# Third token block of six MLP passes by seven half-width products, inverses for two groups, another order of the attention stage

## The chip, the cores and the metric

One core of a Trainium2 chip runs the whole program in one launch. The metric is device time in microseconds, the median of several runs. The profile is one execution of the same program, with its own time.

## The reference

Inputs are q, k, v (2 batches, 8 heads, 768 positions, 64 features each), and weights of two MLPs over 1536 tokens of width 512 with 2048 hidden features. All is float32.

```
k_sum, v_sum: maximum of k and mean of v over blocks of 32 positions
scores = concat(q k^T / 8 where |i - j| < 16 else -1e9,  q k_sum^T / 8 + log 32)
a = softmax(scores);  attn = a @ concat(v, v_sum)
x = attn as (1536 tokens, 512)
h = x @ w_in;   x = (max(h, 0) + alpha * min(h, 0)) @ w_out        # first MLP
h = x @ w_in2;  out = (h * sigmoid(h)) @ w_out2                    # second MLP
```

## The kernel before

**Numbers.** Every float32 operand of the MLPs is held as a high part and a low part (fp32r), and a product is three matmuls: low times high, high times low, high times high (`three`, lines 295 to 302). The weights arrive in a packed form and are turned into these parts by three VectorE bit operations (`bits`, L135 to L151), a ScalarE cast (`w_high`, L162) and a subtraction (`w_low`, L167).

**Stages.** The attention stage takes 24 groups, each one of six blocks of 256 tokens and one of four head pairs. Per group: scores (TensorE, L592), masking and scaling (VectorE, L604), the row maximum (L615), exponentials with row sums (ScalarE, L622), the inverse of the sums (L631 and L632), normalisation (GpSimd, L638), a transpose (TensorE, L644), its copy out of PSUM (L393), the product with the values (L661) and the split of the result into high and low parts (L686, L690). Per batch and head pair it also needs the block maximum of k (L512) with copies of it (L393), and the block means of v: for batch 1 a VectorE sum (`sum_v`, L528).

The MLP stage is eight passes: two layers of four chunks of 512 hidden features. Pass 1 works beside the attention stage, in blocks of 256 tokens. Passes 2 to 8 work on three blocks of 512 tokens. Two of the three take part in a product scheme with seven products in place of eight (`product`, L250 to L282): the contraction (512 features in 4 tiles) is cut in two, a pair of feature tiles is cut in two, and the two token blocks are the third cut. It needs sums of weight pieces (`combine`, L180, `sum_high`, `sum_low`) and sums of token pieces (`x_first` for layer 1, `x_again` for layer 2, cast at L244). Of its partial sums some are copied by ScalarE (`seed_c` L286, `keep` L290) and added by VectorE (`add_to`). The third block (`DIRECT_T`, block 0 in layer 1 and block 2 in layer 2) is computed without it: `direct` (L934) runs four feature tiles of 4 x 3 matmuls of 512 columns. After the activation (L325 and L335, or L341 for the second layer) and its split into high and low (L349, L170) come the output matmuls: `outs` (L988), 12 matmuls for each of four output tiles of a token block, with the running sum put into PSUM by ScalarE before (L417) and copied back after (L438).

**Order.** All instructions are ordered before the launch by `plan` (L1170): every step has an engine, a cost, steps it must follow, buffers it takes and gives, and a key. The planner places the step that can start first, and among those that can start within a small time of each other the one with the lowest key. Steps of the attention stage have keys from the group number and constants (`AT_...`), MLP steps have latest times worked out backwards from TensorE's own order (`late`, L1158). TensorE's MLP steps stand in a list (`line`) and may be moved past two others (`LOOK = 3`). Some steps may go to one of two engines, whichever ends first in the plan. Where the plan has a hole on TensorE early on, dummy matmuls are put in (`fill`, L472).

**Buffers that matter.** Two conversion tiles (`w`), twelve pairs of weight parts (`wt`), four pairs of weight sums (`sw`), seven temporaries (`tmp`), nine pairs of activation parts (`gg`), eight PSUM banks. The weight sums of a pass are given back when the products that read them are done.

The order of TensorE's work from pass 3 on in the kernel before, quoted from lines 1106 to 1112 (`f` is the first feature tile of the third block):

```
def quads(i, f=None, *a):
    for x in ((0, 0), (1, 0), (0, 1), (0, 2), (0, 5), (0, 3), (1, 1), (1, 2),
              (0, 6), (0, 4), (1, 5), (1, 3), (1, 6), (1, 4)):
        if f and x == (1, 5):
            f(*a)
        quad(i, *x)
```

Of the kernel before, what the change touches and what calls it, by code (L numbers as in the profile page):

```python
# [21 lines left out]
P = 128  # L22
# [14 lines left out]
SLACK, RATE = 0.0, 0.28  # L37
# [5 lines left out]
A_PS, A_SB, D_TT, D_STT, D_HALF = 0.5, 0.53, 0.61, 0.69, 0.36  # L43
EARLY, LOOK = {}, 3
NEAR, T_NEAR = {"PE": 0.5, "DVE": 0.2, "ACT": 0.15}, 100.0


@with_exitstack
def tile_blocks_attention_mlps(
# [61 lines left out]
    w_t, sums_t = {}, {}  # L111
# [10 lines left out]
    def temp(name):  # L122
        n = got.pop(0)
        pool, tag = (gpool[0], "mgs"[n]) if n < 3 else (gpool[1], f"t{n}")
        return pool.tile([P, 512], F32, tag=tag, name=name, bufs=1)

# [60 lines left out]

    def sum_high(i, kk, n, at):
        hi = wp2[0].tile([P, 512], F32R, tag="wh", name="sh")
        lo = wp2[0].tile([P, 512], F32R, tag="wl", name="sl")  # L190
        sums_t[i, kk, n] = hi, lo
        nc.scalar.copy(out=hi, in_=w_t[at])

    def sum_low(i, kk, n, at):
        hi, lo = sums_t[i, kk, n]
        less(lo, w_t[at], hi)
# [3 lines left out]
    def pair(l):  # L200
        t = TB * (1 - l)
        return slice(t, t + TB), slice(t + TB, t + 2 * TB)

    def place(l, kk, n):
        if n < 3:
            return tt[0][:, n, 0, kk], tt[0][:, n, 1, kk]
        t1 = pair(l)[1]
# [4 lines left out]
    def x_first(kk, j):  # L212
        t0, t1 = pair(0)
        k2 = kk + KT // 2
        if j == 0:
            for n, tag in enumerate(("wh", "wl", "wh")):
                x_t[kk, n] = wp2[0].tile([P, TB], F32, tag=tag, name="b")
        b11, b12, b22 = [x_t[kk, n] for n in range(3)]
# [11 lines left out]
    def x_again(kk, j):  # L230
        t0, t1 = pair(1)
# [4 lines left out]
    def x_source(l, kk, n):  # L236
        if l == 0:
            return x_t[kk, (0, 2, 1, 0)[n]]
        t0, t1 = pair(1)
# [3 lines left out]
    def x_sum_high(l, kk, n):  # L243
        nc.scalar.copy(out=place(l, kk, n)[0], in_=x_source(l, kk, n))  # L244

    def x_sum_low(l, kk, n):
        hi, lo = place(l, kk, n)
        less(lo, x_source(l, kk, n), hi)

    def product(i, q, n, st):  # L250

        l, ch = passes[i]
        c1, c2 = slice(q * P, (q + 1) * P), slice((q + 2) * P, (q + 3) * P)
        t0, t1 = pair(l)
# [4 lines left out]
        def s(kk, f, c):  # L259
            return tuple(x[:, c] for x in sums_t[i, kk, f])  # L260
# [4 lines left out]
        def t(kk, f):  # L265
            return tt[0][:, f, 0, kk], tt[0][:, f, 1, kk]
# [1094 lines left out]
```

## Time and profile before

| | |
|---|---|
| median of 3 runs | 588.88 us (588.14 to 590.24) |
| the profiled execution | 587.72 us, span 585.9 us |
| TensorE busy | 573.2 us, 98% of the span |
| VectorE busy | 398.2 us, 68% |
| ScalarE busy | 353.4 us, 60% |
| GpSimd busy | 57.3 us, 10%, all before 130 us |
| TensorE clock granted | 1.000 in the mean |

Times in the rows are microseconds from the start of the span. PE is TensorE, PEld its weight loads, DVE VectorE, ACT ScalarE, POOL GpSimd. Durations of matmuls overlap in the trace, so the time that one costs in a stream is read from the starts of two of them.

### The profile page before, as it was taken

The page shows a single profiled execution, that of the slowest core. Times are in us where ns is not written, and L with a number is a line of the kernel's source. Part 1 is how long each engine was busy: PE and PEld are TensorE (multiplying, and loading weights), DVE is VectorE, ACT ScalarE, POOL GpSimd, SP SyncE. Part 2 cuts the span into 40 slices and gives each one's busy share as a digit, 9 for nine tenths or more (in the row PEclk, how much of TensorE's full clock was granted, in tenths as well). Part 3 has the DMA queues.
Part 4 walks back from the last instruction along what each step waited for, and adds up shares of the span by engine and source line. Part 5 has one row for each costly group of instructions (what it writes and reads, how often), then busy time and mean ns, then how long its engine had stood idle before and what let it go on. Part 6 is the DMA issues. An engine that isn't in the chain of part 4 may idle for free.

```text
span 585.9 us, 9240 instructions
## 1 busy us (share of the span) xinstructions
PE 573.2 (98%) x3535; PEld 481.2 (82%) x3535; DVE 398.2 (68%) x711; ACT 353.4 (60%) x781; POOL 57.3 (10%) x64
## 2 busy tenths in 40 slices
PE   8999899999999999999999999999999999999997
PEld 6778778999888888888888788888888888888886
DVE  4889999559999878984799969364657357404110
ACT  3788977436567557654757766436655575646442
POOL 2447644310000000000000000000000000000000
PEclk9999999999999999999999999999999999999999
DMA  8967843200220431242024112240132204000112
GB/s 245 300 212 217 233 136 110 74 1 1 72 73 0 142 110 37 72 148 68 2 78 136 38 37 72 73 143 1 36 109 79 65 0 117 28 1 0 73 54 91
DMA packets 23517, 51.04 MB, mean 87 GB/s; under 512 B 2224, under 2 KB 11696, under 8 KB 23472
## 3 DMA queue, kind: packets, MB, share of 16 engines
q1 hardware_dynamic: 23472, 50.44, 28.4%
q8 instruction: 28, 0.46, 0.3%
q14 instruction: 17, 0.14, 0.1%
HBM read 47.29 MB, written 3.15 MB: 86 GB/s over the span
## 4 chain that ended last, share of the span: by engine, by line
PE 81%; DVE 10%; DMA 4%; ACT 2%; issue 1%; POOL 1%; SPq 0%; ACTq 0%; DVEq 0%
PE ps L298 26%; PE ps L300 26%; PE ps L299 26%; DVE w L146 2%; DMA vs<-in_vw 1%; DMA y<-in_w 1%; DVE nm L615 1%; DVE t L604 1%; PE o L661 1%; DMA cst<-in_consts 1%; DVE w L140 1%; DVE xl L170 1%; DMA kT<-in_kT 1%; PE pt L644 1%; DVE tt L170 1%
## 5 line engine op out<-in xcount | busy, mean ns | idle before, releaser
L170 DVE TENSOR_TENSOR gl<-g,gh 128x512 fp32r<-128x512 f32 x72 | 48.6, 690 | 89.6 <-ACT gh L349 89.2
L298 PE MATMUL ps<-xh,wl 128*128 128x512 f32 (+1 forms) x292 | 104.8, 359 | 1.3 <-ACT ps L286 0.7
L299 PE MATMUL ps<-xl,wh 128*128 128x512 f32 (+1 forms) x292 | 103.4, 354 | 0.0
L300 PE MATMUL ps<-xh,wh 128*128 128x512 f32 (+1 forms) x292 | 103.4, 354 | 0.0
L438 ACT COPY y<-ps 128x512 f32<-128x512 f32 (+1 forms) x81 | 47.2, 582 | 83.1 <-PE ps L300 82.7
L146 DVE SCALAR_TENSOR_TENSOR w<-raw,w 128x512 uint32<-128x512 uint32 x116 | 82.0, 707 | 3.4
L298 PE MATMUL ps<-gh,wl 128*128 128x512 f32 (+1 forms) x240 | 83.6, 348 | 0.6 <-ACT pT L393 0.5
L299 PE MATMUL ps<-gl,wh 128*128 128x512 f32 (+1 forms) x240 | 83.3, 347 | 0.0
L300 PE MATMUL ps<-gh,wh 128*128 128x512 f32 (+1 forms) x240 | 83.2, 347 | 0.0
L299 PE MATMUL ps<-wl,gh 128*128 128x512 f32 (+1 forms) x196 | 75.4, 385 | 0.0
L300 PE MATMUL ps<-wh,gh 128*128 128x512 f32 (+1 forms) x196 | 75.4, 385 | 0.0
L298 PE MATMUL ps<-wh,gl 128*128 128x512 f32 (+1 forms) x196 | 75.4, 385 | 0.0
L298 PEld LDWEIGHTS ps<-xh,wl 128*128 128x128 f32 x292 | 55.1, 189 | 10.8 <-POOL wl L167 1.1
L300 PEld LDWEIGHTS ps<-xh,wh 128*128 128x128 f32 x292 | 55.1, 189 | 7.6
L299 PEld LDWEIGHTS ps<-xl,wh 128*128 128x128 f32 x292 | 55.2, 189 | 7.5
L162 ACT CAST wh<-w 128x512 fp32r<-128x512 f32 x64 | 39.2, 621 | 23.0 <-DVE w L146 22.9
L167 DVE TENSOR_TENSOR wl<-w,wh 128x512 fp32r<-128x512 f32 x54 | 37.1, 693 | 22.6 <-ACT wh L162 21.7
L298 PEld LDWEIGHTS ps<-gh,wl 128*128 128x128 f32 x240 | 45.4, 189 | 6.7 <-ACT pT L393 0.7
L299 PEld LDWEIGHTS ps<-gl,wh 128*128 128x128 f32 x240 | 45.4, 189 | 5.8
L300 PEld LDWEIGHTS ps<-gh,wh 128*128 128x128 f32 x240 | 45.4, 189 | 5.6
L349 ACT CAST gh<-g 128x512 fp32r<-128x512 f32 x72 | 43.5, 621 | 6.5 <-DVE g L335 5.3
L299 PEld LDWEIGHTS ps<-wl,gh 128*128 128x128 f32 x196 | 36.8, 188 | 7.4
(104 smaller groups left out, 962.2 us busy)
## 6 DMA issues: line engine op xcount, KB each, us to landing
raw<-in_w SPq DMA_DIRECT2D x58, 512.0 KB, 3.5
vs<-in_vw SPq DMA_DIRECT2D x16, 288.0 KB, 6.1
kT<-in_kT SPq DMA_DIRECT2D x8, 480.0 KB, 6.3
q<-in_qT SPq DMA_DIRECT2D x24, 128.0 KB, 4.6
y<-in_w SPq DMA_DIRECT2D x6, 512.0 KB, 5.0
out<-y SPq DMA_DIRECT2D x11, 256.0 KB, 2.0
raw<-in_vT SPq DMA_DIRECT2D x4, 384.0 KB, 5.3
cst<-in_consts SPq DMA_DIRECT2D x1, 348.0 KB, 4.9
```

What stands on the lines that cost most here:

```text
L140: nc.vector.tensor_scalar(out=w_t[n], in0=high, scalar1=3, scalar2=0x3FFFFFFF, op0=ALU.logical_shift_left, op1=ALU.bitwise_and,)
L146: nc.vector.scalar_tensor_tensor(out=w_t[n], in0=in0, scalar=scalar, in1=w_t[n], op0=op0, op1=ALU.bitwise_or)
L162: nc.scalar.copy(out=hi, in_=w_t[n])
L167: eng.tensor_tensor(out=lo, in0=w_t[n], in1=hi, op=ALU.subtract)
L170: nc.vector.tensor_tensor(out=out, in0=a, in1=b, op=op)
L298: i = nc.tensor.matmul(ps, all_, bh, start=first, stop=False, skip_group_check=again)
L299: nc.tensor.matmul(ps, ah, bl, start=False, stop=False, skip_group_check=again)
L300: nc.tensor.matmul(ps, ah, bh, start=False, stop=last, skip_group_check=again)
L349: nc.scalar.copy(out=gh, in_=acts_t[u, f])
L438: nc.scalar.copy(out=out_at(u, m, h, halves), in_=out_ps[u, m, h][:, :u[3] // halves])
L604: nc.vector.scalar_tensor_tensor(out=t.rearrange("p (h i) c -> p h (i c)", h=2), in0=s_t.pop((blk, p))[:, :, :2 * NC], scalar=scale, in1=m ...
L615: nc.vector.tensor_reduce(out=nm, in_=t_t[blk, p], axis=AX.X, op=ALU.max, negate=True)
```

## The change

**Third block.** In passes 3 to 8 (`THIRD`) the third block of 512 tokens goes by the seven products as well: it is cut into two halves of 256 columns, which take the place of the two token blocks. There are two row pairs of feature tiles, called products 2 and 3 in `quad`. Pass 2 keeps `direct`. The token sums are formed a second time for the halves (`tt1`), at the start of each layer. Copies, adds and activations of these products are 256 wide; the split into high and low parts is again 512 wide.

**Weight sums.** They are now in use until the third block's products are done. Of the second of each pair of sums only one half has a buffer of its own (256 columns); the other half is written over a piece of the weights that no product reads.

**Order of TensorE.** The two row pairs of the third block stand in `alone`, with output groups between their products. The last output group of a pass (three of them at the change of layer) moves among the first products of the next.

**Buffers.** Temporaries 7 to 5, activation pairs 9 to 8; the activation of the first layer works in place.

**Attention.** From the fifth group on, the inverse of the row sums is taken for two groups at once (24 reductions and 24 reciprocals become 14 and 14). The block sum of v may run on GpSimd as five additions, and does so for three of the four. `PLACES` gives a key to each step of many classes (53 lists, up to 24 entries each) in place of the formula, and `ENGINE` fixes the engine of many steps that had a choice: all eight copies of the k maxima go to GpSimd, 14 copies of transposed scores to ScalarE and 6 to VectorE, the rest stay open.

The core of the diff (most of the two tables, the passing on of `third` and changed planner costs are left out):

```diff
+NTMP, NGG = 5, 8
+LAG = {"POOL": 0.1, "DVE": 0.03}
...
+PLACES = {
+    "k": (
...
+    "e": (
+        38.07, 61.03, -116.39, 46.01, 95.72, 20.52, -16.7, 5.24, -10.94, 41.76, 34.66, 72.25, 132.07, 21.46,
+        -21.38, -35.41, 336.4, 198.65, 371.54, -22.07, 18.91, 95.51, 226.45, 21.33,
+    ),
+    "pt": (
...
+ENGINE = {
+    ("K", "POOL"): (
+        0, 1, 2, 3, 4, 5, 6, 7,
+    ),
...
+    ("vr", "POOL"): (
+        0, 2, 3,
+    ),
+    ("vr", "DVE"): (
+        1,
+    ),
...
+        if n == 0:
+            hi = wp2[0].tile([P, 512], F32R, tag="wh", name="sh")
+            lo = wp2[0].tile([P, 512], F32R, tag="wl", name="sl")
+            sums_t[i, kk, n] = [(hi[:, h], lo[:, h]) for h in HALVES]
+            whole_t[i, kk] = hi, lo
+            nc.scalar.copy(out=hi, in_=w_t[at])
+            return
+        hi = wp2[0].tile([P, 256], F32R, tag="vh", name="sh")
+        lo = wp2[0].tile([P, 256], F32R, tag="vl", name="sl")
+        spare = tuple(x[:, HALVES[1]] for x in pieces[(*passes[i], 0, kk)])
+        sums_t[i, kk, n] = [(hi, lo), spare]
+        for (hi, _), h in zip(sums_t[i, kk, n], HALVES):
+            nc.scalar.copy(out=hi, in_=w_t[at][:, h])
...
+    def pair(l, third=0):
+        t, w = (2 * TB * l, TB // 2) if third else (TB * (1 - l), TB)
+        return slice(t, t + w), slice(t + w, t + 2 * w)
...
         l, ch = passes[i]
+        third, q = divmod(q, 2)
         c1, c2 = slice(q * P, (q + 1) * P), slice((q + 2) * P, (q + 3) * P)
-        t0, t1 = pair(l)
+        t0, t1 = pair(l, third)
...
+    def act_part(u, f, part):
+        if got:
+            acts_t[u, f] = temp("g")
+        return acts_t[u, f][:, part]
...
+            if eng is nc.vector:
+                nc.vector.tensor_reduce(out=t, in_=v, axis=AX.X, op=ALU.add)
+            else:
+                half, part = BLOCK // 2, kv.tile([P, NB, BLOCK // 2], F32, name="vp", bufs=1)
+                while half:
+                    to = part[..., :half] if half > 1 else t.unsqueeze(2)
+                    nc.gpsimd.tensor_tensor(out=to, in0=v[..., :half], in1=v[..., half:2 * half], op=ALU.add)
+                    half, v = half // 2, part
...
+        def inverse(groups, sm):
+            n = 4 * len(groups)
+            rs = att.tile([P, 8, 1], F32, tag="rs", name="rs", bufs=3)
+            r = rs.rearrange("p u o -> p (u o)")[:, :n]
+            at = 4 * sm[1]
+            nc.vector.tensor_reduce(out=r, in_=sm[0][:, at:at + n], axis=AX.X, op=ALU.add)
             nc.vector.reciprocal(out=r, in_=r)
-            sums[blk, p] = rs
+            for j, g in enumerate(groups):
+                sums[g] = rs[:, 4 * j:4 * j + 4]
...
+            twin = (k - SOLO) % 2 if k >= SOLO else 0
+            sm = eps[k // 2 % 3], k % 2
+            mate = order[k - 1] if twin else g
...
+            if k < SOLO:
+                step(("rs", *g), "DVE", 0.28, [("ex", *g)], k + AT_NORM, inverse, [g], sm)
+            elif twin:
+                step(("rs", *mate), "DVE", 0.3, [("ex", *mate), ("ex", *g)], k + AT_NORM, inverse, [mate, g], (sm[0], 0))
+            if k % 2:
+                freed[k // 2 % 3] = mate
...
+            wp2.append(ctx.enter_context(tc.tile_pool(name="wp2", bufs=CF // 2)))
             gpool.append(ctx.enter_context(tc.tile_pool(name="g2", bufs=2)))
-            tt.append(
-                ctx.enter_context(tc.tile_pool(name="tt", bufs=1)).tile([P, 3, 2, KT // 2, TB], F32R, name="tt")
-            )
+            rest = ctx.enter_context(tc.tile_pool(name="tt", bufs=1))
+            for third in range(2):
+                tt.append(rest.tile([P, 3, 2, KT // 2, TB // (1 + third)], F32R, name=f"tt{third}"))
...
+        THIRD = {i: int(i > 1) for i in range(len(passes))}
...
+        def quads(i, left=()):
+            left = dict(zip(((1, 5), (0, 5), (0, 2)), left))
             for x in ((0, 0), (1, 0), (0, 1), (0, 2), (0, 5), (0, 3), (1, 1), (1, 2),
                       (0, 6), (0, 4), (1, 5), (1, 3), (1, 6), (1, 4)):
-                if f and x == (1, 5):
-                    f(*a)
+                if x in left:
+                    outs(*left[x])
                 quad(i, *x)
+
+        def alone(i, q, t, m):
+            for part, order_ in enumerate(((0, 5), (1, 2, 6, 3), (4,))):
+                for n in order_:
+                    quad(i, q, n)
+                if part < 2:
+                    outs(i, t, m, fs=((0, CF // 2), (CF // 2, CF)), part=part)
 
         def some(i, t, *ms):
             for m in ms:
@@ -1118,36 +1417,32 @@
         quads(1)
         split_outs(1, 1)
         some(1, 1, 2, 3)
-        some(1, 2, *range(KT))
+        some(1, 2, *range(KT - 1))
+        left = [(1, 2, KT - 1)]
         for i in range(2, len(passes)):
-            d = DIRECT_T[i]
-            quads(i, direct, i, d, 0)
-            split_outs(i, int(d == 0))
-            if d == 0:
-                some(i, 1, 2)
-                direct(i, 0, 1)
-                some(i, 1, 3)
-                direct(i, 0, 2)
-                direct(i, 0, 3)
-                some(i, 2, 0)
-                some(i, 0, *range(KT))
-                if i == NCH - 1:
-                    token_sums(1)
-                some(i, 2, *range(1, KT))
+            l = passes[i][0]
+            ta, tb, td = (0, 1, 2) if l else (1, 2, 0)
+            quads(i, left)
+            split_outs(i, ta)
+            alone(i, 2, ta, 2)
+            some(i, ta, 3)
+            alone(i, 3, tb, 0)
+            if i == NCH - 1:
+                split_outs(i, td)
+                some(i, td, *range(KT // 2, KT))
+                token_sums(1)
+                token_sums(1, 1)
+                left = [(i, tb, m) for m in (3, 2, 1)]
                 continue
-            some(i, 0, 2, 3)
-            direct(i, d, 1)
-            some(i, 1, 0, 1)
-            direct(i, d, 2)
-            direct(i, d, 3)
-            some(i, 1, 2, 3)
-            if (i, 2) != END:
-                some(i, 2, *range(KT))
+            some(i, tb, *range(1, KT))
+            if (i, td) != END:
+                some(i, td, *range(KT - 1))
+                left = [(i, td, KT - 1)]
                 continue
-            split_outs(i, 2)
-            some(i, 2, *range(KT // 2, KT - 1))
+            split_outs(i, td)
+            some(i, td, *range(KT // 2, KT - 1))
             for h in range(2):
-                outs(i, 2, KT - 1, h, 2)
+                outs(i, td, KT - 1, h, 2)
...
+        seen, moves = {}, {}
+        only = {(c, i): e for (c, e), at in ENGINE.items() for i in at}
+        for x in steps:
+            if x[2] not in moves:
+                c = x[2] if isinstance(x[2], str) else x[2][0]
+                i = seen[c] = seen.get(c, -1) + 1
+                moved = PLACES.get(c, ())
+                moves[x[2]] = moved[i] if i < len(moved) else None, only.get((c, i))
+        steps = [
+            (x[0] if moves[x[2]][0] is None else moves[x[2]][0], *x[1:])
+            for x in steps if moves[x[2]][1] in (None, x[3])
+        ]
```

## Rows read from the trace of the kernel before

**Rows 1.** The page's first part: busy time, share of the span, instructions.

```profile
PE 573.2 (98%) x3535; PEld 481.2 (82%) x3535; DVE 398.2 (68%) x711; ACT 353.4 (60%) x781; POOL 57.3 (10%) x64
```

**Rows 2.** Stretches: length, each engine's busy time, clock granted, DMA share, GB/s.

```profile
24.00:42.00 18.00, 15.83 (x208) 13.12 (x206) 15.14 (x33) 14.27 (x56) 9.56 (x12) 1.00 0.74 226
42.00:79.00 37.00, 33.55 (x486) 27.94 (x484) 36.17 (x82) 32.25 (x117) 22.55 (x24) 1.00 0.76 220
79.00:100.00 21.00, 20.44 (x227) 18.63 (x228) 19.86 (x42) 15.56 (x50) 10.38 (x11) 1.00 0.39 127
140.00:200.00 60.00, 60.00 (x301) 51.05 (x300) 56.57 (x99) 39.06 (x72) 0.00 (x0) 1.00 0.18 54
285.00:306.00 21.00, 21.00 (x93) 17.19 (x92) 18.50 (x32) 14.21 (x26) 0.00 (x0) 1.00 0.17 51
...
301.00:335.00 34.00, 33.35 (x147) 27.32 (x146) 32.76 (x55) 24.07 (x45) 0.00 (x0) 1.00 0.30 88
550.00:586.00 36.00, 32.62 (x156) 27.32 (x154) 2.08 (x3) 13.57 (x26) 0.00 (x0) 1.00 0.20 74
```

**Rows 3.** Order of time near 334 us: start, duration, instruction, idle before.

```profile
334.49 0.50 PE L298 MATMUL ps<-xh,wl 128*128 128x512 f32 x1 [0.65 <-ACT ps L286]
```

**Rows 4.** The chain that ended last: start, duration, what.

```profile
41.89 0.43 DVE w L140
...
78.38 0.58 DVE t L604
```

**Rows 5.** Order of time, TensorE, a hole with dummy matmuls.

```profile
57.96 0.94 PE L472 MATMUL busy<-zero 128*128 128x256 bf16 x7
```

**Rows 6.** Order of time, TensorE, 512 columns: first and last of 19.

```profile
199.77 0.39 PE L299 MATMUL ps<-gl,wh 128*128 128x512 f32 x1
...
203.85 0.39 PE L299 MATMUL ps<-gl,wh 128*128 128x512 f32 x1
```

**Rows 7.** Order of time, TensorE, 256 columns: first and last of 70.

```profile
101.04 0.28 PE L300 MATMUL ps<-xh,wh 128*128 128x256 f32 x1
...
109.32 0.28 PE L300 MATMUL ps<-gh,wh 128*128 128x256 f32 x1
```

**Rows 8.** Groups by form: count, busy us, mean ns; 256 columns wide.

```profile
L170 DVE TENSOR_TENSOR w<-w 128x256 f32<-128x256 f32 x56 | 23.8, 424 | 1.7
...
L417 ACT COPY ps<-y 128x256 f32<-128x256 f32 x2 | 0.8, 386 | 0.0
```

**Rows 9.** Order of time, VectorE: release of weight sums, low parts.

```profile
288.82 0.69 DVE L170 TENSOR_TENSOR u<-u,ps 128x512 f32<-128x512 f32 x1 [0.23 <-PE ps L300]
...
304.66 0.69 DVE L170 TENSOR_TENSOR sl<-w,sh 128x512 fp32r<-128x512 f32 x1
```

**Rows 10.** Groups by form, VectorE: inverses of row sums, block sums of v.

```profile
L632 DVE RECIPROCAL rs<-rs 128x4 f32<-128x4 f32 x24 | 4.3, 178 | 0.8
...
L528 DVE TENSOR_REDUCE vr<-raw 128x24 f32<-128x768 f32 x4 | 3.8, 943 | 0.0
...
L631 DVE TENSOR_REDUCE rs<-eps 128x4 f32<-128x8 f32 x24 | 3.7, 155 | 4.6 <-ACT e L622 4.5
```

**Rows 11.** Groups by form, GpSimd: normalisation, copies of the k maxima.

```profile
L638 POOL TENSOR_TENSOR e<-e,rs 128x480 f32<-128x480 f32 x24 | 23.7, 989 | 33.1 <-DVE rs L632 26.6 <-ACT kT L393 3.0 <-ACT m L370 1.7
...
L393 POOL COPY kT<-kT 128x144 f32<-128x144 f32 x2 | 0.6, 312 | 0.7 <-DVE rs L631 0.7
```

**Rows 12.** Order of time, VectorE and GpSimd near 127 us.

```profile
126.78 2.38 DVE L170 TENSOR_TENSOR b<-xh,xl 128x512 f32<-128x512 f32 x2
129.08 1.28 DVE L170 TENSOR_TENSOR b<-b,xh 128x512 f32<-128x512 f32 x2
...
126.98 1.62 POOL L385 TENSOR_TENSOR gl<-g,gh 128x512 fp32r<-128x512 f32 x1 [10.75 <-ACT gh L382]
```

**Rows 13.** Groups by form, VectorE, 42 to 79 us: the two largest.

```profile
L615 DVE TENSOR_REDUCE nm<-t 128x4 f32<-128x480 f32 x10 | 6.4, 638 | 0.1
L604 DVE SCALAR_TENSOR_TENSOR t<-sc,cst 128x480 f32<-128x480 f32 x10 | 6.4, 637 | 0.0
```

More of the change, by code (lines that the diff above doesn't have):

```diff
@@ new lines @@
+ENGINE = {
+    ("K", "POOL"): (
+        0, 1, 2, 3, 4, 5, 6, 7,
+    ),
+    ("s0", "ACT"): (
+        0, 3, 6,
+    ),
+    ("s0", "POOL"): (
+        1, 5, 7,
+    ),
+    ("s1", "POOL"): (
+        1,
+    ),
+    ("vr", "POOL"): (
+        0, 2, 3,
+    ),
+    ("vr", "DVE"): (
+        1,
+    ),
+    ("s1", "ACT"): (
+        5,
+    ),
+    ("pT", "ACT"): (
+        0, 1, 4, 5, 7, 9, 11, 12, 14, 17, 18, 20, 21, 23,
+    ),
+    ("pT", "DVE"): (
+        3, 6, 13, 16, 19, 22,
+    ),
+    ("lo", "POOL"): (
+        3, 6, 10, 11,
+    ),
+    ("lo", "DVE"): (
+        7, 8,
+    ),
+    ("a3", "POOL"): (
+        0, 1, 4, 5, 9,
+    ),
+    ("oc", "DVE"): (
+        0, 7, 9,
+    ),
+    ("oc", "ACT"): (
+        1, 2, 3, 4, 10,
+    ),
+    ("a3", "DVE"): (
+        7,
+    ),
+}
@@ L278, in product @@
         if new:
[L279 removed]
+            st["ab"[n // 5]] = bank()[:, :TB // (1 + third)]
         ps = st["acaaabb"[n]]
@@ L888, in put, with pe @@
             more.append([name, engine, cost, list(after), f, a, take, give, due, key, size])
-        def pe(name, n, after, f, *a, take=(), give=(), key=None):
-            cost = n * MM
+        def pe(name, n, after, f, *a, take=(), give=(), key=None, mm=MM):
+            cost = n * mm
             if key is None:
@@ L920, in act @@
             u, l = unit(i, t), passes[i][0]
-            me = (i, t, f)
+            me = (i, t, f) if half is None else (i, t, f, half)
+            w = TB // (1 + (half is not None))
+            part = slice((half or 0) * w, (half or 0) * w + w)
+            first = begun.get((i, t, f))
+            new = begun.setdefault((i, t, f), ("g" if l else "m", *me))
+            take = ["tmp"] * (not first)
+            more_ = [first] if first else []
+            a_ps = A_PS if half is None else A_HALF
@@ L931, in act @@
-            put(("gh", *me), "ACT", A_SB, [("g", *me)], act_high, u, f, take=["gg"])
-            put(("gl", *me), "DVE", D_TT, [("gh", *me)], act_low, u, f, give=[own])
+                put(("g", *me), "ACT", a_ps, [src, *more_], act_silu, u, f, get, part, take=take, give=[bank_])
+            else:
+                put(("m", *me), "ACT", a_ps, [src, *more_], act_m, u, f, get, part, take=take)
+                put(("g", *me), "DVE", D_STT if half is None else 0.4, [("m", *me)], act_g, u, f, get, part, give=[bank_])
@@ L934, in direct @@
+            if half is not None and not first:
+                return
+            done = [("g", *me)] if half is None else [("g", i, t, f, h) for h in range(2)]
+            put(("gh", i, t, f), "ACT", A_SB, done, act_high, u, f, take=["gg"])
+            put(("gl", i, t, f), "DVE", D_TT, [("gh", i, t, f)], act_low, u, f, give=[("tmp", new, 0)])
         def direct(i, t, f, key=None, after=("open",)):
```

453 lines of the change are left out of this document (308 added, 145 removed).

## The prediction

> **What bounds the kernel now.** I read the page's first part, then the stretches, then the chain of waits, and last single instructions in order of time. TensorE is busy 98% of the span [rows 1]. In the stretches behind 100 us it is idle for nothing but 0.65 us near 334 us and 3.4 us at the very end, where the last output leaves [rows 2, 3]; the clock column is 1.00 in every stretch. So behind 100 us each microsecond of matmul that is removed should come off the end, as long as what feeds TensorE keeps up. In front of 100 us it is another matter. From 42 to 79 us VectorE is busy 36.17 of 37.00 us and TensorE 33.55 [rows 2], and the chain of waits runs through VectorE pieces, with short issue gaps, from 41.89 to 78.38 us [rows 4]: there VectorE is the limit and TensorE has holes. Some holes are filled with dummy matmuls that the program puts there [rows 5]; the seven of them in one hole take 0.94 us with the tail, so one is about 0.12 us.
>
> **Matmuls removed in passes 3 to 8.** Before, the third block is 4 feature tiles x 4 k tiles x 3 matmuls = 48 matmuls of 512 columns a pass. After, it is 2 row pairs x 7 products x 2 k tiles x 3 = 84 matmuls of 256 columns. What counts is start to start, since the durations overlap. 512 columns: from 199.77 to 203.85 us are 18 steps, 0.2267 us each [rows 6]. 256 columns: from 101.04 to 109.32 us are 69 steps, 0.1200 us each [rows 7]. So 48 x 0.2267 = 10.88 us become 84 x 0.1200 = 10.08 us: 0.80 us a pass, **-4.8 us** in six passes. The count of multiply columns falls by an eighth, 1.36 us a pass; what each matmul costs whatever its width, 2 x 0.1200 - 0.2267 = 0.0133 us by these rows, takes nearly half of it back. The tile shapes are the same 128x128 weights, and in rows 7 these are reloaded for every matmul too, so I take 4.8 as firm to 0.3.
>
> [...]
>
> **What the products add beside TensorE.** Per pass: 2 copies to seed, 4 copies of partial sums, 4 adds, activations in halves. All are 256 wide: a ScalarE copy of that width takes 386 ns, a VectorE add 424 ns with 56 of them in the trace [rows 8]. That is 6 x 0.39 = 2.3 us on ScalarE and 4 x 0.42 = 1.7 us on VectorE per pass of 62 us. Once per layer come the 256-column token sums: 16 adds (layer 1) or 8 (layer 2) and 8 low parts, 10 and 7 us of VectorE. TensorE hides this as long as VectorE has room: from 140 to 200 us it is busy 56.57 of 60 us [rows 2], yet TensorE never waits there, which means that part of this work is done ahead of need. The temporaries fall from 7 to 5 and the activation pairs from 9 to 8, which costs look-ahead. A lone pair of 256-wide products also has short covers: between product 2 (copied out to U) and product 3 stands product 6, 6 x 0.12 = 0.72 us, against 0.39 us of copy plus the hand-overs. If ScalarE is in the midst of a 0.6 us instruction, TensorE stands 0.2 to 0.5 us, unless another group of products is put between. Twelve such pairs: 0 to 6 us, I take +1.0, near the low end, because the present copies between 512-wide products leave no idle time at all from 140 to 200 us [rows 2].
>
> **The layer change near 335 us.** Before, three output groups of the third token block (36 x 0.2267 = 8.2 us) stood between the last tokens and the products of pass 5. After, they are moved among the first products, so only 3 products (4.1 us) and one group (2.7 us) stand before the first product that needs the token sums of layer 2. VectorE is busy 32.76 of 34.00 us here already, and TensorE waited 0.65 us [rows 2, 3]. Bounds 0 and 4 us, I take +1.0 over before.
>
> **The weight sums.** The two buffers of each sum are now held until the third block's products are done, about 43 us into a pass instead of 21 (84 products' matmuls are 19.0 us, then come output groups and the lone pairs). The next pass's sums are queued behind that: two high and low parts, then the conversion of two more weight tiles (only two conversion buffers exist), their combinations and again high and low parts. The nearest rows: the last product that held the buffers ended at 288.8 us (the add to u waits for it), and the sums ended at 305.35 us, 16.5 us with VectorE nearly full [rows 9]. The cover that remains after the change: 1.4 + 0.7 + six output groups of 2.72 + three products of 1.36 = 22.5 us; 19.8 us at the layer change. So I cost it at nothing, with 6 and 3 us to spare; if the chain lasts longer, TensorE stands at five boundaries.
>
> **The attention stage.** Inverses for two groups: of 24 pairs of a small reduction (155 ns) and a reciprocal (178 ns) 10 go, 3.3 us of VectorE. Three of the four value sums (943 ns) go to GpSimd, 2.8 us [rows 10]. In the stretch from 42 to 79 us lie about half: 5 x 0.333 + 2 x 0.943 = 3.5 us. Against that an inverse now waits for the exponentials of a second group, and the exponentials behind it on ScalarE for their turn; the normalisation on GpSimd, and through it the transpose, comes later by up to one group of exponentials. The rest is another order: keys per step, and a fixed engine for many copies (VectorE keeps at least 6 of 10 copies of the transposed scores). The order can't be priced by rows; its bounds can. It can't give more than TensorE's holes from 24 to 100 us, 2.17 + 3.45 + 0.56 = 6.2 us idle [rows 2] and some 15 dummies of 0.12 us: -8.0 us. DMA sets a limit near the same size, as it is still 0.74 to 0.76 busy from 24 to 79 us [rows 2]. At the other end the order may lose 2 us. I take **-3.0**, a bit less than the 3.5 us that VectorE loses in the stretch where it is the limit.
>
> GpSimd gets three value sums by five additions each and six of the key copies (312 ns each [rows 11]). The trace shows no folded sum; 480 elements take 989 ns there [rows 11], so 744 elements in five pieces 1.5 to 3 us: 6 to 11 us in all. Near 127 us two VectorE additions took 2.38 us together, where a subtraction of 1.62 us ran on GpSimd beside them; the next two took 1.28 us [rows 12]. So a two-operand addition between buffers waits for GpSimd. [...] This speaks against moving work to GpSimd, and it is a rival below.
>
> **The sum.** The profiled execution lasted 587.72 us, of which the span is 585.9. 587.72 - 4.8 - 3.0 + 1.0 + 1.0 = 581.9 us. The median of the three timed runs, 588.88, is 1.16 above the profiled one; on it the forecast is **583.0 us**.
>
> **Rivals.**
> A. The attention stage closes nearly all of TensorE's holes. For it: VectorE alone is the limit from 42 us. Against: DMA. Front -7.0, stalls +0.5: 587.72 - 4.8 - 7.0 + 0.5 + 1.16 = 577.6 us.
> B. GpSimd gives nothing back: its 8 or more us of new work block VectorE where conversions and two-operand additions run, and the order gains nothing. For it: rows 12. Against: the two largest groups of VectorE from 42 to 79 us read PSUM or reduce one operand [rows 13], so they are not of the kind that rows 12 show. Front 0: 586.0 us.
> C. The other side: the weight sums come late. If the chain from the release to the last low part takes 26 us in place of 16.5, TensorE stands 3.5 us at each of four boundaries and 6.2 at the layer change, 20 us: 587.72 - 4.8 - 3.0 + 2.0 + 20 + 1.16 = 603. It decides for slower from about 24 us on, where five waits of 1.5 us or more eat the gain. For it: VectorE is 88% busy from 285 to 306 us and 96% from 301 to 335 us [rows 2], and every conversion behind the sums is held up too. Against: 6 us to spare.
> [...]
>
> **How the numbers follow.** The forecast has 0.50 (its own range 579.5 to 586.5), A 0.18, B 0.17, C 0.10, D 0.05. What a measurement can tell from no change is 0.3%, 1.8 us: faster is below 587.1, slower above 590.6. Faster: nearly all of the forecast, A, D and most of B, 0.82; same: the rest of B and a mild C, 0.10; slower: C, 0.08. The range 575.5 to 589.5 reaches from A with all stalls gone (8.0 us of holes) to B with 3 us more of stalls; it leaves out the rest of C and the last of A.
>
> **What would show it.** Matmuls of the third block at 0.120 us start to start, and passes 3 to 8 shorter by 0.8 us each, show the first step. TensorE idle before the first product that reads a sum, at every boundary, would be C; idle inside the lone pairs, with a ScalarE copy as the releaser, the short covers. From 24 to 100 us TensorE idle plus dummies should be 3 us less, with 14 reductions and 14 reciprocals on VectorE; if VectorE is as busy as now and its additions are longer, B. The prediction is wrong if the gain behind 100 us is not about 3 us, or if the front moves by more than 5 us.

## The result, and the profile after

The changed kernel took 583.26 us in the median of four runs (582.63 to 584.19); the kernel before, run beside it on the same chip, 588.87 us (588.14 to 590.24). The ratio is 0.9903, 95% interval 0.988 to 0.9927. The forecast of 583.0 is 0.3 us off. That is in part luck: two of its terms are not what the chip did, and their errors cancel.

The profiled execution lasted 583.64 us (span 581.9), 4.08 less than that of before, while the medians differ by 5.6: the profile of before lay 1.15 us under its median, that of after 0.38 above. The page's first part, against [rows 1]: TensorE has 191 more instructions and 6.9 us less busy time, VectorE and ScalarE have 21 and 19 us more to do.

```profile
PE 566.3 (97%) x3726; PEld 486.2 (84%) x3726; DVE 419.0 (72%) x771; ACT 372.0 (64%) x866; POOL 69.2 (12%) x90
```

The stretches of after (length, then busy time and instructions of TensorE, its weight loads, VectorE, ScalarE and GpSimd, then granted clock, DMA share, GB/s), against [rows 2]. The reader is to see the two front stretches: VectorE falls by 0.5 and 0.7 us only, GpSimd gains 4 and 5 us, TensorE is no busier than before, and the clock is no longer 1.00.

```profile
24.00:42.00 18.00, 15.66 (x233) 12.31 (x231) 14.60 (x29) 15.19 (x57) 13.71 (x21) 0.94 0.88 275
42.00:79.00 37.00, 32.72 (x454) 28.39 (x453) 35.45 (x65) 28.33 (x101) 27.35 (x35) 0.98 0.69 197
79.00:100.00 21.00, 21.00 (x219) 20.22 (x219) 15.89 (x32) 13.92 (x47) 4.48 (x4) 1.00 0.27 77
...
301.00:335.00 34.00, 33.48 (x166) 27.72 (x165) 26.83 (x50) 27.11 (x55) 0.00 (x0) 1.00 0.09 32
```

**A mark splits the kernel in two.** The first TensorE matmul that reads a token sum (`tt` by `sl`, in pass 2) is the same work in both programs. It starts at 168.94 us before and at 168.40 after: all that lies ahead of it, the attention stage and pass 1 above all, gave 0.54 us. From the mark to the start of the last matmul are 413.41 us before (to 582.35) and 409.86 after (to 578.26): 3.55 us. Together these are the 4.09 that the profiles differ by.

```profile
168.94 0.39 PE L298 MATMUL ps<-tt,sl 128*128 128x512 f32 x1
398.71 0.39 PE L298 MATMUL ps<-tt,sl 128*128 128x512 f32 x1
523.83 0.39 PE L298 MATMUL ps<-tt,sl 128*128 128x512 f32 x1
582.35 0.28 PE L300 MATMUL ps<-wh,gh 128*128 128x256 f32 x1
```

Those were TensorE's rows of before, in order of time (start, duration, instruction); the next are the same places of after. Passes 6 and 7 together, second to third row, take 125.12 us before and 123.81 after.

```profile
168.40 0.39 PE L554 MATMUL ps<-tt,sl 128*128 128x512 f32 x1
393.93 0.39 PE L554 MATMUL ps<-tt,sl 128*128 128x512 f32 x1
517.74 0.39 PE L554 MATMUL ps<-tt,sl 128*128 128x512 f32 x1
578.26 0.28 PE L556 MATMUL ps<-wh,gh 128*128 128x256 f32 x1
```

**Where the front's gain stayed.** VectorE's groups from 24 to 79 us, first of before, then of after (count, busy us, mean ns, idle before). Inverses and value sums shrink as planned, from 7.5 to 3.4 us. But the bit operations that unpack the weights, which the change does not touch, take 18.0 us for 20 in place of 13.8 for 21. The saving of 4.1 us pays for 4.2 us of slower work.

```profile
L146 DVE SCALAR_TENSOR_TENSOR w<-y,w 128x512 uint32<-128x512 uint32 x10 | 7.5, 750 | 0.3
L528 DVE TENSOR_REDUCE vr<-raw 128x24 f32<-128x768 f32 x3 | 2.8, 943 | 0.0
L146 DVE SCALAR_TENSOR_TENSOR w<-raw,w 128x512 uint32<-128x512 uint32 x4 | 2.8, 692 | 0.1
L140 DVE TENSOR_SCALAR w<-y 128x512 uint32<-128x512 uint32 x5 | 2.7, 537 | 0.4 <-DMA y<-in_w 0.4
L632 DVE RECIPROCAL rs<-rs 128x4 f32<-128x4 f32 x14 | 2.5, 178 | 0.5
L631 DVE TENSOR_REDUCE rs<-eps 128x4 f32<-128x8 f32 x14 | 2.2, 155 | 1.5 <-ACT e L622 1.4
L140 DVE TENSOR_SCALAR w<-raw 128x512 uint32<-128x512 uint32 x2 | 0.8, 418 | 0.0
```

```profile
L381 DVE SCALAR_TENSOR_TENSOR w<-y,w 128x512 uint32<-128x512 uint32 x10 | 9.5, 951 | 0.3
L381 DVE SCALAR_TENSOR_TENSOR w<-raw,w 128x512 uint32<-128x512 uint32 x4 | 4.1, 1025 | 0.1
L375 DVE TENSOR_SCALAR w<-y 128x512 uint32<-128x512 uint32 x4 | 2.9, 724 | 0.0
L375 DVE TENSOR_SCALAR w<-raw 128x512 uint32<-128x512 uint32 x2 | 1.5, 755 | 0.0
L891 DVE RECIPROCAL rs<-rs 128x8 f32<-128x8 f32 (+1 forms) x7 | 1.4, 199 | 0.2
L890 DVE TENSOR_REDUCE rs<-eps 128x8 f32<-128x16 f32 (+1 forms) x7 | 1.1, 157 | 1.9 <-ACT e L879 1.9
L779 DVE TENSOR_REDUCE vr<-raw 128x24 f32<-128x768 f32 x1 | 0.9, 942 | 0.0
```

Single instructions of after show the place (order of time, VectorE, then GpSimd): a bit operation and a pair of them take 1.07 and 2.54 us while GpSimd ends a normalisation (33.53 to 34.52 us) and a small job and then runs a folded value sum from 34.83 to 38.28 us.

```profile
33.73 1.07 DVE L375 TENSOR_SCALAR w<-y 128x512 uint32<-128x512 uint32 x1
34.84 2.54 DVE L381 SCALAR_TENSOR_TENSOR w<-y,w 128x512 uint32<-128x512 uint32 x2
37.30 0.64 DVE L861 SCALAR_TENSOR_TENSOR t<-sc,cst 128x480 f32<-128x480 f32 x1
```

```profile
34.83 1.01 POOL L784 TENSOR_TENSOR vp<-raw 128x384 f32<-128x384 f32 x1
35.91 2.05 POOL L784 TENSOR_TENSOR vp<-vp 128x192 f32<-128x192 f32 x3
38.05 0.23 POOL L784 TENSOR_TENSOR vr<-vp 128x24 f32<-128x24 f32 x1
```

Behind them stands the masking of the next scores, `t`, and TensorE waits 2.10 us for it. The plan put fewer dummies into the front than before (26 in place of 51), none in this hole. What follows on TensorE is slower: scores at 39.73 us take 1.03 us where those at 38.00 took 0.64, and from 39.70 to 42.80 us the granted clock is 0.52 in the mean (0.50 from 39.83 us on, 1.00 before that).

```profile
35.22 0.69 PE L921 MATMUL o<-pT,vs 120*64 120x64 f32 x16
38.00 0.64 PE L849 MATMUL sc<-kT,q 64*64 64x120 f32 x16 [2.10 <-DVE t L861]
...
39.73 1.03 PE L849 MATMUL sc<-kT,q 64*64 64x120 f32 x16
40.69 1.11 PE L904 MATMUL pt<-cst,e 128*120 128x128 f32 x4
41.73 1.12 PE L921 MATMUL o<-pT,vs 120*64 120x64 f32 x16
```

### The profile page after: what moved, and what is told of

Same layout as the page of the kernel before. It is cut to its first block, busy times and chain, and to the rows that moved or that the text cites. A ratio compares the mean times of both kernels' runs of the same rounds, so it can differ in the third digit from the quotient of the medians.

```text
span 581.9 us, 9753 instructions
## 1 busy us (share of the span) xinstructions
PE 566.3 (97%) x3726; PEld 486.2 (84%) x3726; DVE 419.0 (72%) x771; ACT 372.0 (64%) x866; POOL 69.2 (12%) x90
## 4 chain that ended last, share of the span: by engine, by line
PE 84%; DVE 8%; DMA 4%; ACT 2%; issue 1%; SPq 0%; POOL 0%; DVEq 0%; ACTq 0%
PE ps L554 27%; PE ps L555 27%; PE ps L556 27%; DMA q<-in_qT 2%; DVE w L381 2%; DMA vs<-in_vw 1%; PE o L921 1%; DVE t L861 1%; PE pt L904 1%; PE sc L849 1%; DVE nm L872 1%; DVE w L375 1%; DVE xl L950 1%; DVE g L626 1%; ACT y L688 0%
## 5 line engine op out<-in xcount | busy, mean ns | idle before, releaser
L688 ACT COPY y<-ps 128x512 f32<-128x512 f32 (+1 forms) x85 | 49.4, 582 | 70.1 <-PE ps L556 70.0
L405 DVE TENSOR_TENSOR gl<-g,gh 128x512 fp32r<-128x512 f32 x84 | 56.6, 690 | 49.5 <-ACT gh L599 48.5
L554 PE MATMUL ps<-xh,wl 128*128 128x256 f32 (+1 forms) x268 | 87.6, 327 | 0.0
L555 PE MATMUL ps<-xl,wh 128*128 128x256 f32 (+1 forms) x268 | 86.5, 323 | 0.0
L556 PE MATMUL ps<-xh,wh 128*128 128x256 f32 (+1 forms) x268 | 86.4, 322 | 0.0
L554 PEld LDWEIGHTS ps<-xh,wl 128*128 128x128 f32 x268 | 50.8, 189 | 6.5 <-issue 0.5
L555 PEld LDWEIGHTS ps<-xl,wh 128*128 128x128 f32 x268 | 50.8, 190 | 5.2
L556 PEld LDWEIGHTS ps<-xh,wh 128*128 128x128 f32 x268 | 50.8, 189 | 3.9
L599 ACT CAST gh<-g 128x512 fp32r<-128x512 f32 x84 | 50.4, 619 | 2.9 <-DVE g L590 2.1
L879 ACT ACTIVATE e<-t,nm 128x120 f32<-128x120 f32 x96 | 36.7, 384 | 13.9 <-DVE nm L872 12.6
```

The lines of the kernel that those rows point to most:

```text
L405: nc.vector.tensor_tensor(out=out, in0=a, in1=b, op=op)
L554: i = nc.tensor.matmul(ps, all_, bh, start=first, stop=False, skip_group_check=again)
L555: nc.tensor.matmul(ps, ah, bl, start=False, stop=False, skip_group_check=again)
L556: nc.tensor.matmul(ps, ah, bh, start=False, stop=last, skip_group_check=again)
L599: nc.scalar.copy(out=gh, in_=acts_t[u, f])
L688: nc.scalar.copy(out=out_at(u, m, h, halves), in_=out_ps[u, m, h][:, :u[3] // halves])
```

## The experiments

Each was timed beside the kernel before; "after" is the changed kernel, and "the mark" is the one above. Medians are compared through ratios where the chips differ.

**One half at a time.** The first kernel has the attention stage, order and engine choices of before and the third block of after. The second has the attention stage of after and the MLP of before.

```diff
 # against the kernel after: the third block alone
-PLACES = {
...
-ENGINE = {
...
 # the functions of the attention stage and the planner's loop as before
```

> The attention stage of the kernel before (its keys, its inverses, its engines) with the third block by seven products. If the matmuls give 4.8 us and the waits behind 130 us take 1.2 us of it, as the trace of the changed kernel adds up, this is 3 to 4 us faster than before, and TensorE's starts behind 130 us add up to 0.5 to 3 us over their nominal steps. If the median difference of 5.6 us comes from the products alone, it is 5 us or more faster. If the new order of the attention stage is needed to feed the first passes, it is less than 2 us faster, with waits before 250 us.

```diff
 # against the kernel after: the attention stage alone
-        def quads(i, left=()):
+        def quads(i, f=None, *a):
...
-        def alone(i, q, t, m):
...
 # third block by direct(), the functions of the MLP as before
```

> The MLP passes of the kernel before with the new attention stage (inverses for two groups, value sums on GpSimd, keys and engines from the tables). My forecast was 3.0 us faster for this part alone. By the trace of the changed kernel, where the first product of pass 2 that reads a sum starts 0.54 us earlier, it is 0 to 1 us faster, with the hole near 36 us and the lower granted clock behind it. If the order is worth what the medians leave over (5.6 - 3.6), it is 2 us faster.

The third block alone: 586.34 us (583.89 to 589.0) against 587.93, ratio 0.9969 [0.9952, 0.9986], 1.6 us faster where 3 to 4 were expected. From its mark (170.60 us) to its last matmul (580.20) are 409.6 us, 3.8 less than before: this part is worth what after shows. But its mark is 1.7 us later than that of before, with the same order of the front.

The attention stage alone: 588.02 us (586.81 to 589.57), ratio 0.9989 [0.9974, 1.0003]. Mark at 168.83 us in place of 168.94. The new front gives nothing that can be measured.

**The third block alone, loaded again**, because the late mark had no cause in the program:

> The kernel of e1_third_only once more, loaded anew. There the passes behind 170 us were 3.8 us shorter than before, but the front ended 1.66 us later than before with the same order of instructions, as the first transfers landed later (270 GB/s from 8 to 24 us against 297). If that belongs to one load of a program, the front now ends as before and the kernel is 3.5 to 4 us faster than before; if it goes with this program, it is 1.5 to 2.5 us faster again.

584.45 us (583.62 to 586.72) against 588.72, ratio 0.9928 [0.9901, 0.9956]; mark at 169.41, last matmul at 579.09: 409.68 us between. The stretch behind the mark repeats to 0.1 us; the front does not. From 8 to 24 us the transfers moved 270 GB/s in the first load, 290 in the second, 297 in the profile of before. I take the 4.3 us of the second load as the better value for this part, as its front ended closer to that of before; a difference of a microsecond or two ahead of 100 us can't be read from one load. The same holds for after itself, loaded again:

> The changed kernel itself beside the others on one chip, so that they can be compared with it: 5 to 6 us faster than before if the first measurement holds, 4 us if the profiled executions tell it better; granted clock 0.997 again.

583.06 us (581.62 to 587.54), ratio 0.9911 [0.9879, 0.9944]. The profiled execution was the slowest of the six, 587.54 us. Its mark lies at 172.23 us, 3.8 later than in the first load; from there to the last matmul are 409.94 us, as in the first load. So nearly all of the 3.9 us between these two executions lies in the front. The granted clock was 0.50 there from 23.69 to 27.11 and from 40.76 to 47.59 us.

**The hole filled.** Fourteen dummy matmuls stand ahead of the tenth scores, the one that waits 2.10 us. VectorE and GpSimd do what they did.

```diff
+            n_scores.append((blk, p))
+            if len(n_scores) == 10:
+                fill(14)
```

> The changed kernel with 14 dummy matmuls ahead of the tenth scores, where TensorE stands 2.1 us near 36 us. If the idle hole is what lowers the granted clock, the clock stays at 1.00 in all stretches and the small matmuls from 39.7 to 43 us lose their 0.3 to 0.45 us each, 1.3 us in all. If TensorE is the limit there the end moves by 1.3 us; if VectorE is, later holes take it back and the end moves by less than 0.5 us.

581.55 us (580.99 to 582.51), ratio 0.9881 [0.9862, 0.99], 1.5 to 1.7 us less than after, where 1.3 or less than 0.5 were expected. Loaded again:

> The kernel of e3_hole_filled once more, beside the other two on one chip: 1.3 to 1.8 us faster than the changed kernel (583.1 to 583.3 us), 581 to 582 us.

582.51 us (581.89 to 583.34), ratio 0.9875 [0.9844, 0.9907], 0.5 us above what was expected; before took 589.59 beside it. In the trace of the first load the dummies take 1.70 us of the hole, and the scores behind it take 0.64 us each (order of time, TensorE). The mark is at 166.29 us, 2.1 ahead of after, and at 167.26 in the second load. Against the 583.1 to 583.3 us of after the dummies return 0.6 to 1.7 us by medians and 1.3 to 2.1 by ratios, while the intervals overlap. The tenth scores still wait for `t` (0.47 us behind the dummies); what changes is the clock behind them, 1.00 from 39.4 to 42.5 us in the first load. Three of the six runs of the second load show a mean clock of 0.996 or 0.997 even so: this hole is not the only place where it falls.

```profile
35.58 1.70 PE L722 MATMUL busy<-zero 128*128 128x256 bf16 x14
37.75 0.64 PE L854 MATMUL sc<-kT,q 64*64 64x120 f32 x16 [0.47 <-DVE t L866]
...
39.47 0.64 PE L854 MATMUL sc<-kT,q 64*64 64x120 f32 x16
```

**Three holes filled**, ahead of the fifth, tenth and fourteenth scores:

```diff
+            fill({5: 10, 10: 14, 14: 10}.get(len(n_scores), 0))
```

> The changed kernel with 10, 14 and 10 dummy matmuls ahead of the 5th, 10th and 14th scores, where TensorE stands 1.6, 2.1 and 1.4 us. If every long hole can lower the clock in some executions, the spread of the times shrinks and the median is 581 to 582 us, at a clock of 1.00 in all. If the dummies delay scores that VectorE waits for, it is 0.5 to 2 us slower than with the one hole filled.

581.27 us (580.26 to 584.03), ratio 0.9864 [0.9831, 0.9896]; mark at 164.99 us in the profile, 3.95 ahead of before. The median is what was expected; the spread did not shrink, and two of the six runs, 583.08 and 584.03 us, still had a mean clock of 0.997. It has the lowest ratio of the versions that compute all of the reference; its interval overlaps those of after and of one filled hole.

**The folded sums taken away.** One GpSimd memset stands in for each of the three folds. It leaves out the means of v in batch 1 for three of four head pairs.

```diff
-                while half:
-                    to = part[..., :half] if half > 1 else t.unsqueeze(2)
-                    nc.gpsimd.tensor_tensor(out=to, in0=v[..., :half], in1=v[..., half:2 * half], op=ALU.add)
-                    half, v = half // 2, part
+                nc.gpsimd.memset(t, 0.0)
```

> The changed kernel, same order of steps, but each of the three folded value sums on GpSimd is one memset of the result in place of five additions: the means of v in batch 1 are left out for them. If GpSimd's additions block VectorE's bit operations (1.07 and 2.54 us in place of 0.43 and 1.42 near 34 us), these return to 0.43 and 1.42, the 2.1 us hole on TensorE shrinks below 0.6 us, the clock stays at 1.00 and the end comes 1 to 3 us earlier. If VectorE's long bit operations have another cause (the two tiles that they read, or the DMA), they stay long and the end does not move.

580.35 us (580.05 to 580.62), ratio 0.9859 [0.9841, 0.9877]. The three bit operations near 34 us, on VectorE in order of time, are back to 0.42 and 1.42 us:

```profile
33.35 0.42 DVE L375 TENSOR_SCALAR w<-y 128x512 uint32<-128x512 uint32 x1
33.80 1.42 DVE L381 SCALAR_TENSOR_TENSOR w<-y,w 128x512 uint32<-128x512 uint32 x2
35.14 0.65 DVE L857 SCALAR_TENSOR_TENSOR t<-sc,cst 128x480 f32<-128x480 f32 x1
```

The next `t` starts at 35.14 in place of 37.30 us, TensorE's hole shrinks from 2.10 to 0.33 us without a dummy, the clock does not fall behind it (0.999 in the mean of the execution, the scores at 35.84 and 37.59 us take 0.64 each), and the mark comes 3.65 us earlier. So in after the folds caused most of the hole, in two ways: one runs beside the pair of bit operations, and the one before it (from 30.78 us) holds up a normalisation, which then meets the first bit operation (it starts at 33.53 us in after, at 30.45 here). Whether the hole is filled with dummies or gone, as here, the low clock behind it is gone too.

**All four value sums on VectorE**, at the places of after:

```diff
-            if eng is nc.vector:
+            if True:
```

> The changed kernel with all four value sums as one reduction each on VectorE, at the same places of the same order. My forecast counted 2.8 us less work on VectorE for the move to GpSimd; if VectorE is only relieved by it, undoing it makes the kernel 1 to 2.8 us slower. If the additions on GpSimd block VectorE's bit operations for as long as they run, undoing it costs VectorE 3 x 0.86 us and gives back 1.75 us near 34 us and more near 45 us: between 0.5 us slower and 2 us faster than the changed kernel, with bit operations at 0.43 and 1.42 us, no 2.1 us hole near 36 us and the clock at 1.00.

583.63 us (582.68 to 585.31), ratio 0.9916 [0.9891, 0.994]: the same as after. The bit operations near 34 us are back to 0.44 and 1.42 us, but a reduction now stands ahead of `t`, a hole of 1.73 us stays, and the clock falls behind it (0.56 in the mean from 38.3 to 42.2 us), against what was expected. VectorE's groups from 24 to 79 us: the sums take 2.9 us more than in after, the bit operations 15.3 us for 19 in place of 18.0 for 20.

```profile
L381 DVE SCALAR_TENSOR_TENSOR w<-y,w 128x512 uint32<-128x512 uint32 x9 | 7.7, 859 | 0.3
L381 DVE SCALAR_TENSOR_TENSOR w<-raw,w 128x512 uint32<-128x512 uint32 x4 | 3.9, 974 | 0.1
L779 DVE TENSOR_REDUCE vr<-raw 128x24 f32<-128x768 f32 x4 | 3.8, 946 | 0.0
L375 DVE TENSOR_SCALAR w<-y 128x512 uint32<-128x512 uint32 x4 | 2.3, 574 | 0.0
L375 DVE TENSOR_SCALAR w<-raw 128x512 uint32<-128x512 uint32 x2 | 1.4, 704 | 0.0
```

From the start to 79 us each of the kernels has 24 of these bit operations: they take 15.6 us before, 21.1 in after and 19.2 here. So the folds account for 1.9 of the 5.5 us by which they became longer, and 3.6 stay without any fold. What is left are meetings with GpSimd work that is not folds, in the new order: here a pair takes 2.08 us beside a normalisation, which takes 1.45 in place of 0.99 (VectorE, then GpSimd), as it does in after. That is read from the traces; no run keeps the new order and takes these meetings away.

```profile
53.17 2.08 DVE L381 SCALAR_TENSOR_TENSOR w<-y,w 128x512 uint32<-128x512 uint32 x2
53.26 1.45 POOL L898 TENSOR_TENSOR e<-e,rs 128x480 f32<-128x480 f32 x1
```

**The joint inverses taken apart**, with the order and the places of after:

```diff
-            r = rs.rearrange("p u o -> p (u o)")[:, :n]
-            at = 4 * sm[1]
...
+            for j in range(len(groups)):
+                r = rs.rearrange("p u o -> p (u o)")[:, 4 * j:4 * j + 4]
+                at = 4 * sm[1] + 4 * j
+                nc.vector.tensor_reduce(out=r, in_=sm[0][:, at:at + 4], axis=AX.X, op=ALU.add)
+                nc.vector.reciprocal(out=r, in_=r)
```

> The changed kernel, same order and same waits, but a joint inverse is written as two reductions and two reciprocals again: 20 more small VectorE instructions, 3.3 us. In the run without folded sums 2.6 us less VectorE work moved the end by 2.7 us, so if VectorE is the limit of the whole front, this is 2 to 3.3 us slower than the changed kernel. If only the stretch from 42 to 79 us is limited by it (five of the ten pairs), it is 1 to 1.7 us slower. If the joint inverses only save what other waits hide, less than 0.5 us.

582.75 us (582.28 to 584.13), ratio 0.9885 [0.9856, 0.9914]: no slower than after. But the front ran otherwise in the profiled execution: the hole at this place was 1.43 us, the clock did not fall behind it (1.00 from 38 to 42.8 us), and the mark came at 167.49 us, 0.9 ahead of after. So the ten pairs of instructions that the joint form saves show no gain here; one of the size of the clock's share, 1 to 2 us, could be hidden.

**Less cover for the weight sums.** In passes 3, 5, 6 and 7 the second lone pair of products, which holds the sum buffers, is moved behind three output groups (8.2 us). The work is the same.

```diff
+            late_ = i != NCH - 1
+            if late_:
+                some(i, tb, *range(1, KT))
...
-            some(i, tb, *range(1, KT))
```

> The changed kernel with the second lone row pair of the third block moved behind three output groups (passes 3, 5, 6 and 7), so that the weight sums are released 8.2 us later: the cover to the next product that reads them falls from 22.5 to 14.3 us. In the trace of the changed kernel the chain from release to the last low part that this product needs lasts 15.0, 12.5, 15.4 and 15.6 us at these four boundaries. If that chain is fixed, TensorE stands 0.7 + 0 + 1.1 + 1.3 = 3 us in all and the kernel is 3 us slower than the changed one. If the conversions queued behind the sums also come late (rival C), it is 6 us or more slower. If the chain only looks long because nothing asks for it sooner, nothing changes.

588.29 us (586.41 to 589.7), ratio 0.9988 [0.997, 1.0006]: 5.2 us slower than after on the same chip, between the 3 us and the 6 us that were expected. From the mark to the last matmul are 414.1 us in place of 409.86. Its mark lies at 169.70 us, 1.3 later than in after, with the same front. At three of the four boundaries, for 0.53, 0.81 and 0.83 us, TensorE stands before the sums are even read: the partial sum that a product is seeded with (`ps`) is copied by ScalarE, and ScalarE's next instruction is the cast of a weight sum that VectorE has not combined yet (order of time, ScalarE, then TensorE, at the first of the three). The remaining 2 us of the 4.2 are in shorter delays.

```profile
268.44 0.62 ACT L431 CAST sh<-w 128x512 fp32r<-128x512 f32 x1 [1.41 <-DVE w L405]
268.96 0.58 ACT L542 COPY ps<-ps 128x512 f32<-128x512 f32 x1
```

```profile
269.59 0.50 PE L554 MATMUL ps<-xh,wl 128*128 128x512 f32 x1 [0.53 <-ACT ps L542]
```

## Why the prediction was right, point by point

**Matmuls, -4.8: right.** A product of the third block runs from 229.78 to 231.21 us, 12 matmuls at 0.119 us, as in [rows 7]. Behind the mark 3.55 us went, and 3.8 with the third block alone; with the delays below added back this is 4.8. Passes 6 and 7 are 1.31 us shorter together, with their delays.

**Lone pairs, +1.0, and layer change, +1.0: half of the size, by another mechanism.** Taken as the excess of each start-to-start over 0.2267 or 0.1200 us, TensorE lost 1.34 us behind 127 us before and 2.53 after, so +1.2 in place of +2.0. The layer change holds one real wait in either kernel; in after it is the only one that the trace lists behind 127 us, and no longer than before [rows 3]. It costs nothing. Nor do the lone pairs wait for ScalarE's copies: inside the products of the third block TensorE lost 0.2 us in all. The other 1.0 us lies where I priced nothing, in the output matmuls right behind such a product. The six 512-wide ones that start at 231.21 us take 1.39 us to the next start, in place of 6 x 0.2267 = 1.36, and the same is found at all 36 places where 512-wide matmuls follow 256-wide products, at 1.38 or 1.39 us. No wait is listed there, and why the first wide matmuls behind narrow ones take longer was not tried. That it comes to the +1.0 priced for the copies is chance. The rows of TensorE in order of time: a product, the output matmuls behind it, the next product, and last the wait at the layer change.

```profile
229.78 0.28 PE L554 MATMUL ps<-xh,wl 128*128 128x256 f32 x1
...
231.21 0.40 PE L554 MATMUL ps<-gh,wl 128*128 128x512 f32 x1
...
232.60 0.28 PE L554 MATMUL ps<-xh,wl 128*128 128x256 f32 x1
...
334.48 0.50 PE L554 MATMUL ps<-tt,sl 128*128 128x512 f32 x1 [0.53 <-ACT u L546]
```

**Weight sums, 0: right, and the margin was real.** The last matmul of pass 7 that holds the buffers starts at 495.10 us, the last low part ends at 511.14 (the pair that starts at 510.11), the first use is at 517.74: 16.0 us, 6.6 to spare, where 16.5 and 6 were forecast. Four boundaries measured so took 12.8 to 16 us. At the layer change it is 21.5 us to the sums that the first product reads, and 1.3 us are left there, where 3 were forecast. Rival C's mechanism is there: with 8.2 us less cover the kernel loses 4.2 us behind the mark. Its door is another than I named: ScalarE's queue, ahead of the sums themselves.

```profile
510.11 1.03 DVE L405 TENSOR_TENSOR sl<-w,sh 128x512 fp32r<-128x512 f32 x2 [0.23 <-ACT sh L431]
```

**Attention stage, -3.0: the step that failed.** The trace gives 0.54 us, and the attention stage alone, timed, nothing. I wrote that it would gain "a bit less than the 3.5 us that VectorE loses in the stretch where it is the limit". VectorE lost 0.72 us there and 0.54 from 24 to 42. Over the whole front, the test that the prediction set, TensorE's idle time and dummies from 24 to 100 us, went from 6.2 + 1.7 to 6.6 + 0.2 us: 1 us less in place of 3. Rival B named a cause and I gave it 0.17, because the two largest groups of that stretch are not of the kind that waits for GpSimd [rows 13]. They kept their 0.64 us. The bit operations were of that kind. Their largest group was third by size, and all four together, 9.6 us from 42 to 79 us, are more than either of those two; I had left them out.

The traces show what such meetings cost uint32 operations: the bit operation with one operand took 0.42 us with the folds taken away and 1.07 beside a normalisation in after, the pair with two operands 1.42 and, beside a fold in after, 2.54. From 140 to 200 us of before, where GpSimd does nothing, the same operations take 424 and 691 ns each in the mean (VectorE's groups).

```profile
L146 DVE SCALAR_TENSOR_TENSOR w<-raw,w 128x512 uint32<-128x512 uint32 x14 | 9.7, 691 | 0.4
...
L140 DVE TENSOR_SCALAR w<-raw 128x512 uint32<-128x512 uint32 x8 | 3.4, 424 | 0.1
```

B is not the whole of it. The work moved to GpSimd explains 1.9 of the 5.5 us in longer bit operations; the rest came with the new order, which I had taken as a gain of unknown size. Work saved on VectorE counted where it stood ahead of what TensorE waits for, 2 us at 34 us; for the inverses no gain was seen. And the order left holes without dummies, which cost time through the clock: with every fold in place, filling one hole gave back 0.6 to 2.1 us, and with three filled the mark came 3.95 us ahead of before in the one profile there is, more than the 3.0 forecast. How much of that is the spread between loads is open. Transfers are a rival that no run tests: from 6 to 100 us TensorE waits 3.2 us in all for transfers of q in after, 1.59 of it at once near 20 us; no wait for q is listed before. Ahead of 24 us, which my bounds left out, it is idle for 5.1 us in place of 2.6.

**The step to the median, +1.16: wrong in sign.** The profiled execution of after was 0.38 us above its median. The measured terms, 587.72 - 4.8 - 0.54 + 1.2 = 583.6 us, add up to the 583.64 of the profile, as they must: they are taken from the same two profiles. The forecast for the profile, 581.9, was 1.7 too low, and the step 1.5 too high: that is why 583.0 came out so near.

**What stays open.** By medians the halves give 4.3 (or 1.6 in the other load) and nothing; the whole gives 5.6. Over 1 us of it is in no trace. The front's spread between loads is of this size, and I could not tell whether halves and whole differ by more than that. Nor was it tried what makes transfers land later in some loads, or what an earlier transfer of q would give to the new front.

## What to carry to other kernels

Before work goes from VectorE to GpSimd, look at which VectorE instructions will run beside it, single ones in order of time: if they are two-operand additions or bit operations between SBUF tiles, the gain can be lost there (here a pair of bit operations took 2.54 us in place of 1.42). A new order alone can do the same, where it brings old GpSimd work beside them (here 3.6 of 5.5 us stayed without any fold). Price work that is saved by what waits behind it and not by the busy share of its engine. After a change of order look for idle time on TensorE that dummies used to fill, and for the granted clock just behind it (here 0.50 behind a hole of 2.10 us).

## What the runs showed of the hardware

- A hole of 2.10 us on TensorE was followed by a granted clock of 0.50 from 39.83 to 43.24 us in after, and by one from 40.76 to 47.59 in its second load. With the sums on VectorE a hole of 1.73 us was followed by such a stretch (38.54 to 41.95), and a later one of 1.35 us by another (48.78 to 52.19). A hole of 1.43 us at the first place, with the inverses apart, was not, nor one of 1.44 us near 55 us in after. So the length of a single hole does not tell it here. I had read the clock as settled at 1.00 throughout [rows 2].
- Of one loaded program, the second load of after, runs took 581.62 us at a mean granted clock of 1.000, 582.35 to 583.98 at 0.997, and 587.54 at 0.991. The clock does not explain all of it: at 0.999 to 1.000 the third block alone took 583.62 to 586.72.
- In after the lengthening goes both ways: three of a fold's additions take 1.40 us at 31.87 and at 43.51 us, with no bit operation beside them, and 2.05 us at 35.91 beside a pair of them. In a meeting that two runs share, the instruction that started first kept its time: in after the normalisation at 33.53 us took 0.99 and the bit operation at 33.73 took 1.07, with the inverses apart the bit operation at 33.82 took 0.42 and the normalisation at 33.84 took 1.24.
- In after six 512-wide matmuls take 1.38 or 1.39 us right behind a 256-wide product, at 36 places, and 1.36 elsewhere.
